# Attention, gated layer and PReLU layer in one launch on one core: the first transfer cut in three, weight sums and low parts placed elsewhere at the attention's end, and the activation written as c + (1 - alpha) max(-c, 0)

## The chip, the cores and the metric

The kernel runs on one core of a Trainium2 chip (trn2). The metric is the device time of one launch in microseconds. In the texts PE is TensorE, ACT is ScalarE, DVE is VectorE, POOL is GpSimd and SP is SyncE, which here only issues transfers.

## The reference

For 2 batches of 12 heads, 448 positions and 64 features each, it computes soft-capped attention, then a gated layer with an RMS norm in front, then a layer with a PReLU, all in float32:

```python
scores = cap * tanh(scale * q @ k.T / cap)
attn = exp(scores - max) / (sum(exp) + 1e-9)
x = (attn @ v)                                  # 896 tokens x 768
xn = x / sqrt(mean(x * x) + 1e-6) * rms_g
x = (silu(xn @ w_gate) * (xn @ w_val)) @ w_out  # 768 -> 1536 -> 768
h = x @ w_in                                    # 768 -> 2048
g = max(h, 0) + alpha * min(h, 0)               # alpha: one number per feature
out = g @ w_out2                                # 2048 -> 768
```

## The kernel before

Each float32 matmul operand of the two layers is split in two float32r tiles, a high part (`wh`, `xh`, cast by ACT) and a low part (`wl`, `xl`, value minus high part, by DVE). A product is then three matmuls: high by high, low weight by high, high weight by low. The matmuls of a layer's first half (L344, and L356 for two weight groups at once) are 128x128 by 128x448.

The first matrix of each layer is multiplied by a seven-product (Strassen-Winograd) scheme. For every weight group g there are products P1 to P7, with the weights A11, A12, A22 and the sums S1 = A21 + A22, S2 = S1 - A11, S3 = A22 - S2, S4 = A12 - S2 (`sum1` to `sum4`, POOL, L115), and the operands B11, B21, B22, T1 to T4 (sums of quarters of the activations, on DVE). A weight tile arrives by an SP transfer into one of 3 `raw` buffers, ACT makes `top` of it (`w_top`, L103), DVE puts both together (`w_bits`, L107), and only then may SP load the next tile into that buffer (`w_next`). `w_hi` (L120, ACT) and `w_lo` (L124, DVE) split a weight.

The order of the work is written out by hand, each engine runs its own list in order, and waits are semaphores. There are four parts:

- The attention (L364 to L451) runs over 12 pairs of heads, 4 steps each: `qk` (PE, L199), `soft` (ACT, L209 and L210), `pv` (PE, L225 and L229). The first pair's queries and keys come in two transfers (L375) and are split by ACT (L386) and DVE (L387 to L389) as they land. DVE then makes the constants `cinv` and `eps_t` (L390 to L396), on which the first `tanh` waits.
- The attention's end (L466 to L490). `recip` makes the reciprocals of the last softmax sums as a high and a low part (`th` L271, `tl` L272), SP spreads each into the tile `r` (L279). `norm` broadcasts them by a matmul into `rps` (L286), DVE scales the attention's output with it (L288, L289), and ACT and POOL sum the squares (L298, L300). `rms` sums them over the partitions (`ms`, L309), and DVE takes the reciprocal root (L313). Between these PE runs P1 and P2 (`product`) of the first two groups of the gated layer, which need batch 0 alone. Then `by_tiles` (L520 to L534) makes T1 in three tiles of 448 columns: `xnorm` (L326), a subtraction, a cast by ACT (L527) and the low part.
- The layers, slot by slot. A slot is one product; the list `hooks` says what the other engines do after its matmuls are issued. The gated layer starts with P5 of groups 0 and 1 together (L356), then P6, P7, P3, P4 of the two groups, one group after the other. Two PSUM pairs of the pool `s` and two of the pool `m` take turns, so P5 and P6 are each in a pair of their own, P7 adds onto P6's after `u2` has read it, and P3 adds onto P5's after `add22` has read it (both are DVE L508).
- The second layer (z) has the PReLU: `prelu_a` makes max(-c, 0) (ACT, L822) and multiplies each half by its alpha (ACT, L825, two instructions), and `prelu_b` takes max(c, 0) minus that (DVE, L828, one instruction of 128x896). Its output goes through `ksplit` (L756 and L508) into the last matrix (f: L593, L595, L597).

Of the kernel before, what the change touches and what calls it, by code (L numbers as in the profile page):

```python
# [56 lines left out]
def attn_moe_kernel(ctx: ExitStack, tc: tile.TileContext, units, qk_in, v, sel, w, gvec, alpha, cap, out):  # L57
# [304 lines left out]
    with tc.manual_schedule():  # L362
# [17 lines left out]
        for t, src in ((g_t, gvec), (al_t, alpha)):  # L380
            nc.sync.dma_start(out=t, in_=src)
        r = raw.pop(0)
        for h, (c0, c1) in enumerate(cuts):
            qc = slice(0, S) if h == 0 else slice(QK - S, QK)
            kc = slice(S, QA) if h == 0 else slice(QA, QK - S)
            nc.scalar.copy(hi[0][:, qc], r[:, qc])  # L386
            nc.vector.tensor_copy(hi[0][:, kc], r[:, kc])  # L387
            nc.vector.tensor_tensor(out=hi[0][D:, kc], in0=r[D:, kc], in1=hi[0][D:, kc], op=ALU.subtract)  # L388
            nc.vector.tensor_tensor(out=q2[0][:, h], in0=r[:, qc], in1=hi[0][:, qc], op=ALU.subtract)  # L389
        nc.vector.reciprocal(out=cinv, in_=cap_t)  # L390
        nc.vector.tensor_scalar_mul(cinv, cinv, QK_SCALE)

# [78 lines left out]
        w_hi(("g", 0, "S1"))  # L471
        w_lo(("g", 0, "S1"))
        first_sum(0, ct("c21"))
        product(pa[1], ("g", 1, "A11"), "B11", True, rows=(0,))
        norm(last - 1)
        norm(last)
        product(pa[1], ("g", 1, "A11"), "B11", True, rows=(1,))
        product(pa[0], ("g", 0, "A12"), "B21", False, rows=(0,))
        w_hi(("g", 1, "S1"))
        rms(B - 1)  # L480
        first_sum(1, ct("c21"))
        c11 = [spare[B - 1][:, :2], xpool.tile([P, 2, S], F32, tag="B22l", name="c11")]
# [24 lines left out]
        def tt(out, a, b, op):  # L507
            nc.vector.tensor_tensor(out=out, in0=a, in1=b, op=op)  # L508
# [8 lines left out]
        def operand_low(name, src):  # L517
            tt(oper[name][1], src, oper[name][0], ALU.subtract)

        def by_tiles(name, i0, out, a, b, fn=None, *args):  # L520

            h, l = (main.tile([P, K3, S], F32R, tag=f"{name}{p}", name=f"x{p}") for p in "hl")
            low = lambda k: tt(l[:, k], out[:, k], h[:, k], ALU.subtract)
            for k in range(K3):
                xnorm(i0 + k)
                tt(out[:, k], a[:, k], b[:, k], ALU.subtract)
                nc.scalar.copy(h[:, k], out[:, k])  # L527
                if k == 1 and fn:
                    fn(*args)
                if k > 0 and not fn:  # L530
                    low(k - 1)
            for k in range(0 if fn else K3 - 1, K3):
                low(k)
            oper[name] = (h, l)  # L534

        i1 = (B - 1) * NP
        by_tiles("T1", i1, x0[:, lo3], x1[:, lo3], x0[:, lo3], w_lo, ("g", 1, "S1"))
        w_hi(("g", 1, "S2"))


# [11 lines left out]
        def pslot(lay, p, g):  # L552

            first = p in ("P1", "P6", "P5")
            wn, xn = OPER[p]

            def pe():
                if first:
                    BANK[p][g] = psum()
                if lay == "g" and p == "P5" and g < 2:  # L560
                    if g == 1:
                        products([pc[0], pc[1]], [("g", 0, "S1"), ("g", 1, "S1")], "T1")
                    return
# [157 lines left out]
            gate(at_["P3"] + 2, g, 1, c12)  # L721


        for g in range(2):
            do(g, 2, w_lo, ("g", g, "S2"))
            do(1 + g, 4, sum3, "g", g)
            do(3 + g, 4, sum4, "g", g)
        do(0, 0, by_tiles, "T2", i1 + K3, x0[:, lo3], x1[:, hi3], x0[:, lo3])

        def later_operands(n0, steps):  # L730
            for name, at_sum, at_hi, out, a, b in steps:
# [72 lines left out]
                        ("B22", 0, 5, b22, None, None), ("T4", 4, 6, b21, b21, b11)))  # L804


        def z_of(g, q):
            if g not in zt:
                zt[g] = block(g)
            return zt[g][:, 2 * q:2 * q + 2, :]  # L810
# [6 lines left out]
            nc.scalar.copy(c11z[g], pa[g][:, :, :S])  # L817

        def prelu_a(g, q, of):
            src, t = of[g][:, :, :S], z_of(g, 0) if q == 0 and g > 1 else (cu if q % 2 else ct)("zn")  # L820
            minus[g, q] = t
            nc.scalar.activation(out=t, in_=src, func=AF.Relu, scale=-1.0)  # L822
            for r in range(2):
                f = q // 2 * (K2N // 2) + 2 * g + r
                nc.scalar.activation(out=t[:, r], in_=t[:, r], func=AF.Copy, scale=al_t[:, f:f + 1])  # L825

        def prelu_b(g, q, of):
            nc.vector.scalar_tensor_tensor(  # L828
                out=z_of(g, q), in0=of[g][:, :, :S], scalar=0.0, in1=minus.pop((g, q)), op0=ALU.max, op1=ALU.subtract
            )  # L830
# [125 lines left out]
```

## Time and profile before

| | |
|---|---|
| median of 3 runs | 611.1 us (610.14 to 617.62) |
| the profiled execution | 616.38 us, of which 614.6 us are the span of its instructions |
| PE busy | 589.5 us, 96% of the span, 2672 matmuls |
| DVE busy | 402.6 us, 66% |
| ACT busy | 357.5 us, 58% |
| POOL busy | 118.7 us, 19% |

The span is the time from the first to the last instruction. A row of a timeline gives the start in us from the span's start, the duration in us, engine, source line, operation, the tile written, the tiles read, the shapes and how many equal instructions are merged; in brackets stands how long the engine was idle before it and what released it. A DVE duration includes time in which the instruction was issued but held up. PE durations overlap, so the rate of matmuls is read from the starts.

### The profile page before, as it was taken

Reading aid. Unit: us, or ns where it says so; the run is one execution under the profiler, and the core shown is the slowest. Engines: PE = TensorE matmul, PEld = TensorE weight load, DVE = VectorE, ACT = ScalarE, POOL = GpSimd, SP = SyncE. Lnnn points to the kernel's source line nnn. Section 1 sums busy time; section 2 is a strip of 40 time slices with the busy share of each in tenths; the row PEclk is TensorE's granted clock in tenths of the full one; section 3 lists DMA queues with packets and bytes.
Section 4 is the critical chain, followed back from the end, with each engine's and each line's share of the span. In section 5 each row is a group of like instructions: output and inputs, shape, how many; then the busy total and the mean of one; then the engine's idle time right before and its main releaser. Section 6 shows DMA issues by size and latency. Waiting matters only on the chain.

```text
span 614.6 us, 6899 instructions
## 1 busy us (share of the span) xinstructions
PE 589.5 (96%) x2672; PEld 503.7 (82%) x2672; DVE 402.6 (66%) x439; ACT 357.5 (58%) x437; POOL 118.7 (19%) x71
## 2 busy tenths in 40 slices
PE   5999988989899999999999999999989999999997
PEld 4666645667799999999999999999979989999996
DVE  7437689967999867766961545679986877614100
ACT  5999878964755455346562542666776887323101
POOL 0013463235003514411000017210451000000000
PEclk9999999999899999999999999999999999999999
DMA  8664642203014434412344264002341344422002
GB/s 294 255 229 159 262 142 86 78 13 145 1 52 153 156 108 149 155 42 85 131 155 155 102 241 171 0 1 67 138 155 52 103 155 136 172 112 81 1 1 90
DMA packets 18632, 73.47 MB, mean 120 GB/s; under 512 B 5672, under 2 KB 6056, under 8 KB 18600
## 3 DMA queue, kind: packets, MB, share of 16 engines
q1 hardware_dynamic: 15592, 72.82, 33.4%
q0 software_dynamic: 2864, 0.21, 0.4%
q8 instruction: 21, 0.34, 0.2%
q14 instruction: 11, 0.09, 0.0%
q10 hardware_dynamic: 144, 0.00, 0.0%
HBM read 70.14 MB, written 2.75 MB: 119 GB/s over the span
## 4 chain that ended last, share of the span: by engine, by line
PE 69%; DVE 7%; issue 3%; DMA 2%; ACT 2%; POOL 0%; SPq 0%; ACTq 0%; DVEq 0%; POOLq 0%
PE s L344 19%; PE m L344 13%; PE s L597 6%; PE s L595 6%; PE s L593 6%; PE m L593 5%; PE m L595 5%; PE m L597 5%; DVE b L508 2%; DMA r<-tl 1%; DVE wl L124 1%; PE ob L229 1%; PE oa L225 1%; PE s L199 1%; DVE b L828 1%
## 5 line engine op out<-in xcount | busy, mean ns | idle before, releaser
L124 DVE TENSOR_TENSOR wl<-wt,wh 128x768 fp32r<-128x768 f32 x98 | 105.9, 1086 | 94.5 <-ACT wh L120 94.2
L115 POOL TENSOR_TENSOR wt<-wt 128x768 f32<-128x768 f32 x40 | 87.8, 2201 | 256.8 <-DVE wt L107 149.3
L120 ACT CAST wh<-wt 128x768 fp32r<-128x768 f32 x98 | 81.3, 833 | 90.6 <-PE s L595 24.7
L103 ACT CAST top<-raw 128x768 f16<-128x768 bf16 x68 | 72.6, 1075 | 44.8 <-DVE wt L107 38.3
L107 DVE SCALAR_TENSOR_TENSOR wt<-raw,top 128x768 uint32<-128x768 uint32 x68 | 67.8, 999 | 8.0 <-ACT top L103 7.6
L344 PE MATMUL s<-xh,wh 128*128 128x448 f32 x234 | 61.8, 372 | 1.0 <-ACT xh L527 1.0
L344 PE MATMUL s<-xh,wl 128*128 128x448 f32 x234 | 61.5, 371 | 1.1 <-DVE wl L124 1.1
L344 PE MATMUL s<-xl,wh 128*128 128x448 f32 x234 | 61.4, 370 | 0.0
L199 PE MATMUL s<-hi 128*128 128x448 f32 x96 | 49.3, 513 | 7.2 <-DVE hi L388 6.6
L593 PE MATMUL s<-ks,wh 128*128 128x448 f32 x176 | 50.6, 367 | 0.8 <-DVE b L828 0.8
L597 PE MATMUL s<-ks,wl 128*128 128x448 f32 x176 | 50.5, 366 | 0.0
L344 PEld LDWEIGHTS s<-xh,wh 128*128 128x128 f32 x234 | 44.3, 190 | 6.3 <-ACT xh L527 1.4
L344 PEld LDWEIGHTS s<-xh,wl 128*128 128x128 f32 x234 | 44.2, 190 | 5.7 <-DVE wl L124 1.3
L209 ACT ACTIVATE pt<-s,cinv 128x896 f32<-128x896 f32 (+1 forms) x48 | 43.6, 908 | 8.6 <-PE s L199 7.2
L344 PEld LDWEIGHTS s<-xl,wh 128*128 128x128 f32 x234 | 44.3, 190 | 4.4
L344 PE MATMUL m<-xh,wh 128*128 128x448 f32 x174 | 45.4, 369 | 1.6 <-ACT b L464 1.6
L210 ACT ACTIVATE pt<-pt,cap_t 128x896 f32<-128x896 f32 (+1 forms) x48 | 45.6, 950 | 1.6
L593 PE MATMUL m<-ks,wh 128*128 128x448 f32 x160 | 45.8, 368 | 0.5 <-DVE b L508 0.5
L597 PE MATMUL m<-ks,wl 128*128 128x448 f32 x160 | 45.8, 367 | 0.0
L344 PE MATMUL m<-xh,wl 128*128 128x448 f32 x174 | 45.2, 368 | 0.0
L344 PE MATMUL m<-xl,wh 128*128 128x448 f32 x174 | 45.2, 368 | 0.0
L229 PE MATMUL ob<-pt,vt 128*128 128x448 f32 x96 | 41.8, 539 | 0.0
(122 smaller groups left out, 977.9 us busy)
## 6 DMA issues: line engine op xcount, KB each, us to landing
raw<-w_in SPq DMA_DIRECT2D x68, 768.0 KB, 4.4
rw<-qk_in SPq DMA_DIRECT2D x11, 928.0 KB, 5.1
vt<-v_in SPq DMA_DIRECT2D x12, 416.0 KB, 5.7
out<-o SPq DMA_DIRECT2D x5, 448.0 KB, 2.5
rw<-qk_in SPq DMA_DIRECT2D x1, 480.0 KB, 4.5
rw<-qk_in SPq DMA_DIRECT2D x1, 448.0 KB, 5.6
out<-o SPq DMA_DIRECT2D x2, 224.0 KB, 2.0
gt<-ea SPq DMA_DIRECT2D x12, 1.8 KB, 1.7
```

Source lines behind the costliest of these rows:

```text
L103: nc.scalar.copy(top_of[u].bitcast(F16)[:, 1::2], raw_t[u].bitcast(BF16)[:, 4:4 * UW + 4:4])
L107: nc.vector.scalar_tensor_tensor(out=f_t[u].bitcast(U32), in0=raw_t.pop(u).bitcast(U32)[:, 1:2 * UW + 1:2], scalar=13, in1=top_of.pop(u), ...
L115: nc.gpsimd.tensor_tensor(out=t, in0=f_t[a], in1=f_t[b], op=op)
L120: nc.scalar.copy(h_t[u], f_t[u].rearrange("p (k m) -> p k m", m=P))
L124: nc.vector.tensor_tensor(out=l_t[u], in0=f_t[u].rearrange("p (k m) -> p k m", m=P), in1=h_t[u], op=ALU.subtract)
L199: nc.tensor.matmul(s[:, n, :S], hi[i][:, S + o:S + o + P], t[hd], start=(m == 0), stop=(m == len(mm) - 1),)
L210: nc.scalar.activation(out=t[:, :n], in_=t[:, :n], func=AF.Exp, scale=cap_t)
L229: nc.tensor.matmul(ob[i][:, :S], lhs, r, start=(h == "T"), stop=(h == "B" and c == 2))
L344: nc.tensor.matmul(ps[:, r, :S], lhs, rhs, start=first and n == 0, stop=n == len(mm) - 1, skip_group_check=True,)
L593: nc.tensor.matmul(dst[l], wh[:, o, :], xh[l], start=first, stop=False)
L595: nc.tensor.matmul(dst[l], wh[:, o, :], xl[l], start=False, stop=False)
L597: nc.tensor.matmul(dst[l], wl[:, o, :], xh[l], start=False, stop=fin)
```

## The change

1. The first pair's queries and keys come in three transfers: queries and the first 256 key columns of head 0, the next 256, the rest. The second has a cast and a subtraction of its own on DVE.
2. At the attention's end `sum3` of the two groups stands on POOL before the last sum of squares, and `sum4` behind it; both stood behind it before. P1 of group 1 is done whole before the last `norm`. `w_lo` of S1, group 1, stands before the reciprocal root.
3. T1 is made whole before its low parts, which follow as one block. T2's first tile comes next, then `w_lo` of S2 for both groups, then T2's other tiles and its low parts. P6 of groups 0 and 1 is done as a pair, as P5 was.
4. The PReLU is c + (1 - alpha) max(-c, 0): DVE turns alpha into 1 - alpha once, ACT makes max(-c, 0) alone, and DVE does the rest in two instructions of 128x448 with the factor as a pointer.

```diff
-        cuts = [(0, QA), (QA, QK)]
+        K0 = S + 2 * P
+        cuts = [(0, K0), (K0, QA), (QA, QK)]
...
-        for h, (c0, c1) in enumerate(cuts):
-            qc = slice(0, S) if h == 0 else slice(QK - S, QK)
-            kc = slice(S, QA) if h == 0 else slice(QA, QK - S)
-            nc.scalar.copy(hi[0][:, qc], r[:, qc])
+        for kc, h, qc in (((S, K0), 0, slice(0, S)), ((K0, QA), None, None), ((QA, QK - S), 1, slice(QK - S, QK))):
+            kc = slice(*kc)
+            if h is not None:
+                nc.scalar.copy(hi[0][:, qc], r[:, qc])
...
         first_sum(0, ct("c21"))
-        product(pa[1], ("g", 1, "A11"), "B11", True, rows=(0,))
+        for g in range(2):
+            sum3("g", g)
+        product(pa[1], ("g", 1, "A11"), "B11", True)
         norm(last - 1)
         norm(last)
-        product(pa[1], ("g", 1, "A11"), "B11", True, rows=(1,))
+        for g in range(2):
+            sum4("g", g)
         product(pa[0], ("g", 0, "A12"), "B21", False, rows=(0,))
         w_hi(("g", 1, "S1"))
+        w_lo(("g", 1, "S1"))
         rms(B - 1)
...
-                if lay == "g" and p == "P5" and g < 2:
+                if lay == "g" and p in ("P5", "P6") and g < 2:
                     if g == 1:
-                        products([pc[0], pc[1]], [("g", 0, "S1"), ("g", 1, "S1")], "T1")
+                        products([BANK[p][0], BANK[p][1]], [("g", i, wn) for i in range(2)], xn)
                     return
...
-        for g in range(2):
-            do(g, 2, w_lo, ("g", g, "S2"))
-            do(1 + g, 4, sum3, "g", g)
-            do(3 + g, 4, sum4, "g", g)
-        do(0, 0, by_tiles, "T2", i1 + K3, x0[:, lo3], x1[:, hi3], x0[:, lo3])
+        def second_operands():
+            low()
+            one2, low2 = tile_maker("T2", i1 + K3, x0[:, lo3], x1[:, hi3], x0[:, lo3])
+            one2(0)
+            for g in range(2):
+                w_lo(("g", g, "S2"))
+            for k in range(1, K3):
+                one2(k)
+            low2()
+
+        do(0, 0, second_operands)
...
+        do(z0 - 6, 5, lambda: nc.vector.tensor_scalar(
+            out=al_t, in0=al_t, scalar1=-1.0, scalar2=1.0, op0=ALU.mult, op1=ALU.add))
...
         def prelu_a(g, q, of):
-            src, t = of[g][:, :, :S], z_of(g, 0) if q == 0 and g > 1 else (cu if q % 2 else ct)("zn")
-            minus[g, q] = t
-            nc.scalar.activation(out=t, in_=src, func=AF.Relu, scale=-1.0)
-            for r in range(2):
-                f = q // 2 * (K2N // 2) + 2 * g + r
-                nc.scalar.activation(out=t[:, r], in_=t[:, r], func=AF.Copy, scale=al_t[:, f:f + 1])
+            t = minus[g, q] = (cu if q % 2 else ct)("zn")
+            nc.scalar.activation(out=t, in_=of[g][:, :, :S], func=AF.Relu, scale=-1.0)
 
         def prelu_b(g, q, of):
-            nc.vector.scalar_tensor_tensor(
-                out=z_of(g, q), in0=of[g][:, :, :S], scalar=0.0, in1=minus.pop((g, q)), op0=ALU.max, op1=ALU.subtract
-            )
+            t = minus.pop((g, q))
+            for r in range(2):
+                f = q // 2 * (K2N // 2) + 2 * g + r
+                nc.vector.scalar_tensor_tensor(
+                    out=z_of(g, q)[:, r], in0=t[:, r], scalar=al_t[:, f:f + 1], in1=of[g][:, r, :S],
+                    op0=ALU.mult, op1=ALU.add
+                )
```

`tile_maker` is `by_tiles` taken apart: it returns one function that makes a tile (`xnorm`, subtraction, cast) and one that makes the three low parts.

The order of the instructions at three places, before and now. First POOL at the attention's end, before: `s2` is the sum of squares, `wt` a weight sum (the first two are `sum3`, the next two `sum4`).

```order
L277 DMA r2_0_84<-tl_931 4x16x28
L300 TENSOR_TENSOR s2_863<-s2_863,sq_997 128x448
L300 TENSOR_TENSOR s2_863<-s2_863,sq_1008 128x448
L300 TENSOR_TENSOR s2_863<-s2_863,sq_1059 128x448
L115 TENSOR_TENSOR wt_401<-wt_578,wt_239 128x768
L115 TENSOR_TENSOR wt_480<-wt_653,wt_314 128x768
L115 TENSOR_TENSOR wt_750<-wt_750,wt_239 128x768
L115 TENSOR_TENSOR wt_832<-wt_832,wt_314 128x768
```

POOL at the same place now:

```order
L277 DMA r2_0_84<-tl_934 4x16x28
L300 TENSOR_TENSOR s2_866<-s2_866,sq_1000 128x448
L300 TENSOR_TENSOR s2_866<-s2_866,sq_1011 128x448
L115 TENSOR_TENSOR wt_404<-wt_581,wt_242 128x768
L115 TENSOR_TENSOR wt_483<-wt_656,wt_317 128x768
L300 TENSOR_TENSOR s2_866<-s2_866,sq_1073 128x448
L115 TENSOR_TENSOR wt_753<-wt_753,wt_242 128x768
L115 TENSOR_TENSOR wt_835<-wt_835,wt_317 128x768
```

The two `sum3` stand directly behind the second sum of squares.

Next DVE where T2 is made, before: `xl` is a low part (the first row that names it still belongs to T2's own), `wl` is `w_lo` of S2 for the two groups.

```order
L326 SCALAR_TENSOR_TENSOR xf<-xf,g_t,spare 128x448
L508 TENSOR_TENSOR xf<-xf 128x448
L326 SCALAR_TENSOR_TENSOR xf<-xf,g_t,spare 128x448
L508 TENSOR_TENSOR xf<-xf 128x448
L508 TENSOR_TENSOR xl<-xf,xh 128x448
L326 SCALAR_TENSOR_TENSOR xf<-xf,g_t,spare 128x448
L508 TENSOR_TENSOR xf<-xf 128x448
L508 TENSOR_TENSOR xl<-xf,xh 128x448 x2
L124 TENSOR_TENSOR wl<-wt,wh 128x768 x2
```

DVE at the same place now:

```order
L326 SCALAR_TENSOR_TENSOR xf<-xf,g_t,spare 128x448
L514 TENSOR_TENSOR xf<-xf 128x448
L124 TENSOR_TENSOR wl<-wt,wh 128x768 x2
L326 SCALAR_TENSOR_TENSOR xf<-xf,g_t,spare 128x448
L514 TENSOR_TENSOR xf<-xf 128x448
L326 SCALAR_TENSOR_TENSOR xf<-xf,g_t,spare 128x448
L514 TENSOR_TENSOR xf<-xf 128x448
L514 TENSOR_TENSOR xl<-xf,xh 128x448 x3
```

The two `w_lo` moved from the end of the block to behind T2's first tile.

Last DVE in the second layer, before: `zn` is what `prelu_a` made, `b` a block of the layer's output.

```order
L124 TENSOR_TENSOR wl<-wt,wh 128x768
L107 SCALAR_TENSOR_TENSOR wt<-raw,top_86 128x768
L828 SCALAR_TENSOR_TENSOR b_2955<-b_2955,zn 128x896
L508 TENSOR_TENSOR b_2955<-m,b_2955 128x896
L124 TENSOR_TENSOR wl<-wt,wh 128x768
L508 TENSOR_TENSOR b_2927<-s,b_2927 128x896
L828 SCALAR_TENSOR_TENSOR b_2927<-b_2927,zn 128x896
L124 TENSOR_TENSOR wl<-wt,wh 128x768
```

DVE at the same place now:

```order
L124 TENSOR_TENSOR wl<-wt,wh 128x768
L107 SCALAR_TENSOR_TENSOR wt<-raw,top_86 128x768
L844 SCALAR_TENSOR_TENSOR b_2959<-zn,al_t,b_2959 128x448 x2
L514 TENSOR_TENSOR b_2959<-m,b_2959 128x896
L124 TENSOR_TENSOR wl<-wt,wh 128x768
L514 TENSOR_TENSOR b_2931<-s,b_2931 128x896
L844 SCALAR_TENSOR_TENSOR b_2931<-zn,al_t,b_2931 128x448 x2
L124 TENSOR_TENSOR wl<-wt,wh 128x768
```

The order is the same; each PReLU row became two instructions of half the size.

## Rows read from the trace of the kernel before

**Rows 1.** A wait of PE (engine, line, waited for: us, times, longest).

```profile
PE rps L286 <- DMA r<-tl: 4.2, 3, 1.8
```

**Rows 2.** Instructions on the first pair's raw tile: ns min/median/max, first and last start.

```profile
L387 DVE CAST hi<-rw x2: 387/408/429, 5.3 to 7.0; 128x512 fp32r<-128x512 f32 x1, 128x448 fp32r<-128x448 f32 x1
L388 DVE TENSOR_TENSOR hi<-rw,hi x2: 623/656/689, 5.8 to 7.4; 64x512 fp32r<-64x512 f32 x1, 64x448 fp32r<-64x448 f32 x1
```

**Rows 3.** Timeline of the start: the first softmax step.

```profile
9.07 1.01 ACT L209 ACTIVATE pt<-s,cinv 128x896 f32<-128x896 f32 x1 [1.37 <-DVE eps_t L396]
```

**Rows 4.** Timeline of the attention's end: from POOL's second sum to its weight sums.

```profile
133.89 1.15 POOL L300 TENSOR_TENSOR s<-s,sq 128x448 f32<-128x448 f32 x1 [0.80 <-ACT sq L298]
...
134.20 0.88 DVE L271 CAST th<-gt 64x28 fp32r<-64x28 f32 x1
...
135.11 0.18 DVE L272 TENSOR_TENSOR tl<-gt,th 64x28 fp32r<-64x28 f32 x1
...
135.97 0.57 SPq L279 DMA_DIRECT2D r<-tl  x1
...
138.12 0.64 PE L286 MATMUL rps<-r,sel_t 128*128 128x448 f32 x2 [1.80 <-DMA r<-tl]
...
141.71 5.43 POOL L115 TENSOR_TENSOR wt<-wt 128x768 f32<-128x768 f32 x3
```

**Rows 5.** Timeline within the attention: a DVE pair beside POOL.

```profile
91.91 3.39 DVE L179 TENSOR_TENSOR q<-rw,hi 128x448 fp32r<-128x448 f32 x2
...
93.51 1.31 POOL L296 TENSOR_TENSOR sq<-xf 128x448 f32<-128x448 f32 x1
```

**Rows 6.** Timeline of PE: P6 of the first group.

```profile
158.45 0.57 PE L344 MATMUL s<-xh,wh 128*128 128x448 f32 x2
...
161.54 1.49 PE L344 MATMUL s<-xh,wl 128*128 128x448 f32 x3 [1.06 <-DVE wl L124]
```

**Rows 7.** Two windows: us, PE, PEld, DVE, ACT, POOL busy (instructions), PEclk, DMA, GB/s.

```profile
162.00:163.00 1.00, 1.00 (x4) 0.87 (x4) 1.00 (x2) 1.00 (x2) 0.00 (x0) 0.50 0.00 0
420.00:441.00 21.00, 21.00 (x104) 19.22 (x103) 20.93 (x20) 14.45 (x20) 6.99 (x3) 1.00 0.34 113
```

**Rows 8.** Timeline of DVE behind P6: u2 and T3's low part, add22 of group 1.

```profile
166.39 1.09 DVE L508 TENSOR_TENSOR b<-s,c 128x896 f32<-128x896 f32 x1 [0.62 <-PE s L344]
...
168.26 1.55 DVE L508 TENSOR_TENSOR xl<-xf,xh 128x1344 fp32r<-128x1344 f32 x1
...
179.51 1.09 DVE L508 TENSOR_TENSOR c<-m,c 128x896 f32<-128x896 f32 x1
```

**Rows 9.** Timeline of PE: the first matmuls of P3, group 1.

```profile
181.07 0.78 PE L344 MATMUL m<-xh,wh 128*128 128x448 f32 x3
```

**Rows 10.** Timelines: two DVE pieces that price a half PReLU.

```profile
12.89 1.16 DVE L179 TENSOR_TENSOR q<-rw,hi 128x448 fp32r<-128x448 f32 x2
...
150.00 0.68 DVE L326 SCALAR_TENSOR_TENSOR xf<-xf,g_t,spare 128x448 f32<-128x448 f32 x1
```

**Rows 11.** Timeline of the second layer: DVE and POOL side by side.

```profile
431.82 1.09 DVE L828 SCALAR_TENSOR_TENSOR b<-b,zn 128x896 f32<-128x896 f32 x1
432.07 2.55 POOL L115 TENSOR_TENSOR wt<-wt 128x768 f32<-128x768 f32 x1 [30.65 <-ACT top L103]
...
433.82 1.61 DVE L124 TENSOR_TENSOR wl<-wt,wh 128x768 fp32r<-128x768 f32 x1
...
449.50 1.40 DVE L828 SCALAR_TENSOR_TENSOR b<-b,zn 128x896 f32<-128x896 f32 x1 [1.23 <-ACT zn L825]
...
452.76 1.08 DVE L508 TENSOR_TENSOR b<-s,b 128x896 f32<-128x896 f32 x1
```

**Rows 12.** Timeline of PE in the second layer and at the last matrix's start.

```profile
454.06 0.79 PE L344 MATMUL s<-xh,wh 128*128 128x448 f32 x3
...
495.49 0.69 PE L593 MATMUL m<-ks,wh 128*128 128x448 f32 x2 [0.51 <-DVE b L508]
```

**Rows 13.** ACT by line and shape, 400 to 530 us: us busy, mean ns.

```profile
L825 ACT ACTIVATE zn<-zn,al_t 128x448 f32<-128x448 f32 x28 | 17.2, 663 | 0.5
```

More of the change, by code (lines that the diff above doesn't have):

```diff
@@ L382, in attn_moe_kernel @@
         r = raw.pop(0)
-        for h, (c0, c1) in enumerate(cuts):
-            qc = slice(0, S) if h == 0 else slice(QK - S, QK)
-            kc = slice(S, QA) if h == 0 else slice(QA, QK - S)
-            nc.scalar.copy(hi[0][:, qc], r[:, qc])
+        for kc, h, qc in (((S, K0), 0, slice(0, S)), ((K0, QA), None, None), ((QA, QK - S), 1, slice(QK - S, QK))):
+            kc = slice(*kc)
+            if h is not None:
+                nc.scalar.copy(hi[0][:, qc], r[:, qc])
             nc.vector.tensor_copy(hi[0][:, kc], r[:, kc])
             nc.vector.tensor_tensor(out=hi[0][D:, kc], in0=r[D:, kc], in1=hi[0][D:, kc], op=ALU.subtract)
-            nc.vector.tensor_tensor(out=q2[0][:, h], in0=r[:, qc], in1=hi[0][:, qc], op=ALU.subtract)
+            if h is not None:
+                nc.vector.tensor_tensor(out=q2[0][:, h], in0=r[:, qc], in1=hi[0][:, qc], op=ALU.subtract)
         nc.vector.reciprocal(out=cinv, in_=cap_t)
@@ L518, in operand_low, with tile_maker, one @@
             tt(oper[name][1], src, oper[name][0], ALU.subtract)
-        def by_tiles(name, i0, out, a, b, fn=None, *args):
+        def tile_maker(name, i0, out, a, b):
             h, l = (main.tile([P, K3, S], F32R, tag=f"{name}{p}", name=f"x{p}") for p in "hl")
-            low = lambda k: tt(l[:, k], out[:, k], h[:, k], ALU.subtract)
-            for k in range(K3):
+            oper[name] = (h, l)
+            def one(k):
                 xnorm(i0 + k)
@@ L527, in by_tiles, with low @@
                 nc.scalar.copy(h[:, k], out[:, k])
[L528 to L534, printed above, removed]
+            def low():
+                for k in range(K3):
+                    tt(l[:, k], out[:, k], h[:, k], ALU.subtract)
+            return one, low
         i1 = (B - 1) * NP
-        by_tiles("T1", i1, x0[:, lo3], x1[:, lo3], x0[:, lo3], w_lo, ("g", 1, "S1"))
+        one, low = tile_maker("T1", i1, x0[:, lo3], x1[:, lo3], x0[:, lo3])
+        for k in range(K3):
+            one(k)
         w_hi(("g", 1, "S2"))
@@ L819, in prelu_a, with prelu_b @@
         def prelu_a(g, q, of):
-            src, t = of[g][:, :, :S], z_of(g, 0) if q == 0 and g > 1 else (cu if q % 2 else ct)("zn")
-            minus[g, q] = t
-            nc.scalar.activation(out=t, in_=src, func=AF.Relu, scale=-1.0)
+            t = minus[g, q] = (cu if q % 2 else ct)("zn")
+            nc.scalar.activation(out=t, in_=of[g][:, :, :S], func=AF.Relu, scale=-1.0)
+        def prelu_b(g, q, of):
+            t = minus.pop((g, q))
             for r in range(2):
                 f = q // 2 * (K2N // 2) + 2 * g + r
-                nc.scalar.activation(out=t[:, r], in_=t[:, r], func=AF.Copy, scale=al_t[:, f:f + 1])
-        def prelu_b(g, q, of):
-            nc.vector.scalar_tensor_tensor(
-                out=z_of(g, q), in0=of[g][:, :, :S], scalar=0.0, in1=minus.pop((g, q)), op0=ALU.max, op1=ALU.subtract
-            )
+                nc.vector.scalar_tensor_tensor(
+                    out=z_of(g, q)[:, r], in0=t[:, r], scalar=al_t[:, f:f + 1], in1=of[g][:, r, :S],
+                    op0=ALU.mult, op1=ALU.add
+                )
         def prelu(n, g, q, of):
```

## The prediction

> **What bounds the kernel now.** I read the table of busy times first: PE is busy for 589.5 of 614.6 us, so about 25 us of the span are left to waiting, and no edit here removes a matmul. The list of PE's waits comes next: which of them the change touches. One is the broadcast `rps`, three times behind the spread of the reciprocal's low part, 4.2 us in all and 1.8 at the longest [rows 1]; others are single waits of about 1 us at P6 of the gated layer [rows 6]. Then the timelines, stage by stage, for what runs ahead of each wait and how long the work behind it can slip. Last the windows: between 162 and 163 us PE did 4 matmuls at a granted clock of 0.50, while 104 matmuls took 21.0 us at a clock of 1.00 in the second layer, 0.20 each [rows 7]. (0.50 is the lower of the two levels, 1.2 GHz.) So three quantities decide: the wait at `rps`, the gaps and the low clock at P6, and in the second layer DVE, which is busy for 20.93 of the 21 us between 420 and 441 [rows 7] and whose delays reach PE.
>
> All sums are made against the profiled execution, 616.38 us, of which 1.8 us lie outside the span. It is 5.3 us above the median of the runs, 611.1; I work out a difference and put it on the median.
>
> **The start (part 1): 0, between -0.2 and +0.2.** The first `tanh` waits not for PE but for DVE's constant `eps_t`, 1.37 us [rows 3]. That constant is last in a DVE chain that begins, for the second piece, around 7.0 us, when the end of the raw tile has landed [rows 2]. A third transfer doesn't make the last one land earlier; it makes the first piece land earlier, and PE's first matmuls with it, which is not what `tanh` waits for. DVE gets a cast and a subtraction more, of half the size: by row 2 a mean cast is 0.41 and a mean subtraction 0.66, so two halves cost some 0.1 each above one whole. This falls into the time in which DVE waits for the last piece.
>
> **The attention's end (part 2): +0.9, between -0.1 and +1.8.** The wait of 1.80 at `rps` starts because P1 of group 1 was cut in two rows of nine matmuls: nine were kept for behind `norm`. Now they stand ahead, 9 x 0.20 = 1.8 us, which fills the wait exactly. But the same nine are missing behind `rps`, where the sum over partitions waits for DVE's scaling, ACT's square and POOL's sum. PE's work is the same and the chain is the same, so the wait moves and nothing is gained; what counts is when `rps` can run.
>
> That is now later. Before, POOL ended its second sum of squares at 133.89 + 1.15 = 135.04. Beside it DVE's cast `th`, of 28 columns, took 0.88, where the subtraction `tl` of the same size just behind took 0.18 [rows 4]: I read 0.7 of it as a hold until POOL let go, since `th` ended at 135.08. The same shows elsewhere: two instructions that take 1.16 together [rows 10] took 3.39 when POOL's square stood between them [rows 5]. Now two `sum3` stand directly behind that second sum on POOL. When it ends, `th` goes, and the `sum3` that is waiting goes ahead of `tl`. One such sum took 5.43 / 3 = 1.8 us [rows 4]. So `tl` begins near 136.7 instead of 135.11 and ends near 136.8. SP's transfer left 0.68 us after `tl`'s end before; I take it that SP was still busy with the transfer of `th` then, and that it now leaves at once. It reached PE 2.15 us after its start (135.97 to 138.12). So `rps` runs at 136.8 + 2.15 = 139.0, 0.9 later than at 138.12 [rows 4]. If the 0.68 is a fixed delay it is +1.6 to +1.8; if `tl` gets in first, about 0 (-0.1 with POOL's order).
>
> **P6 as a pair (part 3): -0.7, between -1.0 and +1.0.** Before, P6 of group 0 ran from 158.45, with a gap in front of its third matmul and one of 1.06 in front of the fourth, which waited for `w_lo` of S2 [rows 6]. The 15 matmuls left then took from 161.54 to 166.39, when `u2` could start [rows 8]: 4.85 us for what takes 3.1 at the full clock, a loss of some 1.7. With `w_lo` of S2 and T2's first tile made earlier, and two groups' matmuls on every tile, I count the gaps and the low clock as gone. The pair, 36 matmuls at 0.20 to 0.21, ends at about 158.45 + 7.4 = 165.9.
>
> The gain does not stay, because DVE has no gap from `u2` to beyond P3 of group 1. `u2` of group 0 had to wait for P6 of group 0 alone; now that ends with the pair, at 165.9 plus a few tenths, so `u2` starts at about 166.07, 0.32 earlier than at 166.39. P7 of group 0 adds onto what `u2` reads and needs T3's low part for its last six matmuls, which ends at 168.26 + 1.55 = 169.8 less 0.32 [rows 8]. So PE, 4 us ahead after P6, stands still in P7. P3 of group 1 began at 181.07 [rows 9], behind `add22`, which ended at 179.51 + 1.09 = 180.60 [rows 8], a slack of 0.47; now `add22` ends at 180.28 and PE may start 181.07 - 180.28 = 0.79 earlier at most. Less what passes between the two engines I take -0.7. The transition as a whole, parts 2 and 3: +0.9 - 0.7 = +0.2.
>
> **The PReLU (part 4): +1.0, between -0.8 and +2.9.** ACT loses two multiplications of 0.66 per PReLU, 28 of them in its list between 400 and 530 us [rows 13]. DVE gets two instructions of 448 columns instead of one of 1.09 for 896 [rows 11]. No row has the new form; the nearest are a pair of 448 columns that took 1.16 together, and a pointer-scaled one of the same kind that took 0.68 by itself, 1.36 for two [rows 10]. The lower end is +0.07 per PReLU, the upper +0.27; I take +0.2, since the single one has the same operands as the new form.
>
> The Trainium skill has a rule against this edit: "VectorE: DVE Perf Modes", section "The DRAIN you can't avoid", says that after each DVE operation the pipe empties before the next one starts, so one long operation beats two short ones. By it the halves cost 2 x 0.68 and the edit +0.27; the pair of 1.16 speaks for the lower end, and the sum would then be 0.4 smaller over the first five PReLUs.
>
> DVE is full around 430 us, so every PReLU pushes what follows: two of them before 431, +0.4. At 431.82 a PReLU of 1.09 begins, and at 432.07 POOL starts a weight sum of 2.55 [rows 11], which the next large DVE instructions but one then had to share with. With a gap between halves POOL gets in there. Before, from the start of the PReLU to the end of `w_lo` it took 433.82 + 1.61 - 431.82 = 3.6; now a half 0.6, POOL's sum of 1.7 to 1.8, a half 0.5, an addition of 1.0 and `w_lo` 0.95 give 4.75: +1.1. Three more PReLUs add 0.4 to 0.5, so DVE is 1.9 late near 447. There a wait of 1.23 for ACT's multiplication stood before [rows 11]; it goes, but the POOL sum that ran in it now holds DVE instead. I therefore keep the whole 1.9 up to the addition `b<-s`, which ended at 452.76 + 1.08 = 453.84 [rows 11], 0.22 ahead of the matmul at 454.06 that needs it [rows 12]: PE is late by 1.9 - 0.2 = 1.7 or 1.8.
>
> At the last matrix's start ACT, without two multiplications (1.3 us), gives its part earlier. PE waits there for DVE, 0.51 at 495.49 [rows 12] and some 0.8 just before; the first goes, the second in part: -0.8. The sum of this part is 1.8 - 0.8 = +1.0. With DVE taking turns well it is -0.8; with the 0.27 and one more sum in the way, +2.9.
>
> **Sum.** 0 + 0.2 + 1.0 = +1.2, so 617.6 us for the profiled execution and 611.1 + 1.2 = 612.3 us for the median.
>
> **Rivals.**
> - *POOL gets in nowhere.* `tl` and both halves go ahead of the waiting sums. Then part 2 is 0, P6 gives -0.7 and the second layer -0.8: together about -1.4, 609.7 us. For it: POOL's own start after a wait isn't instant, and at 135.11 DVE had `tl` out 0.03 after `th` [rows 4]. Against: rows 5, where POOL came between two DVE instructions that had no wait either. Chance 0.27.
> - *Slower: the low clock moves to P7.* The gaps at P6 are exchanged for gaps in P7, while PE stands behind `u2` and T3's low part between 166 and 169.5. Before, gaps of about 1 us each preceded the stretch at 0.50 [rows 6, 7] and cost 1.7. If the clock falls in P7, P3 of group 1 finds no slack and the -0.7 becomes +1.0; with both `sum3` ahead of `th`, `rps` is 1.8 later again. It decides once PE's standstill in P7 is as long as the two gaps together. 611.1 + 1.2 + 1.7 = 614.0, with the second sum 615.8. Chance 0.17.
> - *More or less than is seen.* A wait in the attention or a transfer moved in the second layer, that the reading missed, of several us either way: 0.06.
>
> The forecast has 0.50. The range is 606.5 to 616.5: the bounds of the unknown costs give -1.7 to +5.7, and below I leave some us for the spread of the runs (610.14 to 617.62) and for P7 finding its operands early. About 2%, 12 us, is what a measurement of this kernel can tell from no change; all cases lie inside. Faster by more than that 0.02, within 0.95, slower 0.03.
>
> **What would show each step.** Start: the first `tanh` within 0.2 of 9.07, still released by `eps_t`. End of attention: `tl` a microsecond or more behind `th`, with a POOL sum between, and `rps` near 139.0; PE idle not before `rps` but before the sum over partitions. P6: no wait in front of its matmuls, 36 in 7.5 us, then PE waiting for `u2` and T3's low part. Second layer: pairs of halves of 1.16 to 1.36, one of them with a POOL sum inside, and PE's matmul of 454.06 near 455.8. I am wrong if `rps` is earlier than 138.12, if P7 starts without a wait, or if the pairs take no more than 1.1.

## The result and the profile after

| | before | after |
|---|---|---|
| median of 20 runs | 615.59 us (610.14 to 618.14) | 618.42 us (614.38 to 624.26) |
| the profiled execution | 616.38 us, span 614.6 | 615.77 us, span 614.0 |
| after against before | | 1.0059, 95% interval 1.0033 to 1.0086 |

The change made the kernel slower by 0.6%, 2 to 5 us. The predicted median, 612.3, and the whole range up to 616.5 lie below the measured one, for two reasons: the 611.1 us on which the difference of +1.2 was put was the median of three runs, and twenty give 615.59; and the difference itself is larger than forecast.

The two profiled executions took nearly the same time, so their spans alone would mislead. This is PE's list of waits in the changed kernel (engine, line, waited for: us, times, longest):

```profile
PE rps L286 <- DMA r<-tl: 5.1, 3, 2.9
...
PE s L344 <- DVE b L514: 2.3, 2, 1.4
...
PE ms L309 <- POOL s L300: 1.2, 1, 1.2
PE m L344 <- ACT b L466: 0.8, 1, 0.8
PE s L344 <- DVE xl L514: 0.8, 1, 0.8
```

The longest wait at `rps` is now 2.9 us, where [rows 1] had 1.8, and it is not the one at the attention's end. I then lined up the two traces softmax step by softmax step. The first `tanh` (9.51 against 9.07, [rows 3]) is 0.44 later; the 25th is at 63.91 against 63.52; the 26th at 71.26 against 66.85. Within one step of the attention, which the diff doesn't touch, 4 us were lost. The timeline of that place in the changed kernel:

```profile
58.74 0.18 DVE L272 TENSOR_TENSOR tl<-gt,th 64x28 fp32r<-64x28 f32 x1
58.85 0.94 DVE L107 SCALAR_TENSOR_TENSOR wt<-raw,top 128x768 uint32<-128x768 uint32 x1
...
59.65 1.33 POOL L277 DMA_DIRECT2D r<-tl  x1
59.72 1.11 DVE L175 CAST hi<-rw 128x1856 fp32r<-128x1856 f32 x1
59.82 0.33 SPq L93 DMA_DIRECT2D raw<-w_in  x1
...
68.27 0.71 PE L286 MATMUL rps<-r,sel_t 128*128 128x448 f32 x1 [2.90 <-DMA r<-tl]
...
71.26 1.01 ACT L209 ACTIVATE pt<-s,cinv 128x896 f32<-128x896 f32 x1 [3.90 <-PE s L199]
```

And in the kernel before:

```profile
57.75 0.18 DVE L272 TENSOR_TENSOR tl<-gt,th 64x28 fp32r<-64x28 f32 x1
...
58.24 0.96 DVE L107 SCALAR_TENSOR_TENSOR wt<-raw,top 128x768 uint32<-128x768 uint32 x1 [0.31 <-ACT pt L209]
...
58.66 0.62 POOL L277 DMA_DIRECT2D r<-tl  x1
...
59.12 1.12 DVE L175 CAST hi<-rw 128x1856 fp32r<-128x1856 f32 x1
59.22 0.33 SPq L93 DMA_DIRECT2D raw<-w_in  x1
...
64.48 0.71 PE L286 MATMUL rps<-r,sel_t 128*128 128x448 f32 x1
```

This is the spread of the second group's reciprocals. POOL issues it as two small transfers, `r<-th` and `r<-tl`. Before, DVE paused 0.31 us between `tl` and the weight instruction L107; POOL was nearly through with `r<-tl` (0.62 us) when DVE's cast of 128x1856 began. Now the pause is gone, the cast begins 0.07 us after POOL's issue did, the issue takes 1.33 us, until 60.98, 0.15 us behind the end of that cast. By then SP, which began at 59.82, is at the last of three large loads; before, POOL's issue ended at 59.28, when SP had begun the first. The list of DMA issues (KB, us from issue to landing) shows what that costs, before:

```profile
r<-tl POOLq DMA_DIRECT2D x1, 7.0 KB, 2.1
```

and after:

```profile
rw<-qk_in SPq DMA_DIRECT2D x1, 928.0 KB, 6.4
raw<-w_in SPq DMA_DIRECT2D x1, 768.0 KB, 4.5
vt<-v_in SPq DMA_DIRECT2D x1, 416.0 KB, 7.0
...
r<-tl POOLq DMA_DIRECT2D x1, 7.0 KB, 8.5
```

The three loads land at 64.34, 66.65 and 67.73, and `r<-tl` behind all of them at 68.14.

The Trainium skill, "SBUF — State Buffer", section "SBUF: two separate sides", describes this: descriptors of a transfer issued by POOL are written by POOL itself, which cannot write them while DVE runs a copy in float32 within SBUF, and a transfer issued by SP is free of it. The trace agrees: 1.33 against 0.62 us for the same issue, and its end just behind the cast's.

The rest is in the main as foreseen in kind. The attention's end in the changed kernel:

```profile
139.35 4.44 POOL L115 TENSOR_TENSOR wt<-wt 128x768 f32<-128x768 f32 x2
...
139.46 1.78 DVE L272 TENSOR_TENSOR tl<-gt,th 64x28 fp32r<-64x28 f32 x1
...
141.27 0.57 SPq L279 DMA_DIRECT2D r<-tl  x1
...
143.37 0.64 PE L286 MATMUL rps<-r,sel_t 128*128 128x448 f32 x2 [0.87 <-DMA r<-tl]
...
147.03 1.02 PE L309 MATMUL ms<-s,ones 128*128 128x448 f32 x2 [1.20 <-POOL s L300]
```

`tl` took 0.18 in [rows 4] and takes 1.78, with POOL's sums beside it, and SP's transfer follows at once. Counted from the last `tanh` (126.89 before, 131.24 after), `rps` comes after 11.23 and now after 12.13 us: +0.90. The sum over partitions `ms` follows 3.66 us behind `rps` and waits for POOL; before it came 4.20 behind, directly after 18 matmuls of P1 and P2 and without a wait:

```profile
142.32 0.91 PE L309 MATMUL ms<-s,ones 128*128 128x448 f32 x2
```

In P7 and in the second layer of the changed kernel:

```profile
170.23 1.09 DVE L514 TENSOR_TENSOR b<-s,c 128x896 f32<-128x896 f32 x1 [1.69 <-PE s L356]
...
171.47 0.85 PE L344 MATMUL s<-xh,wh 128*128 128x448 f32 x3 [0.88 <-DVE b L514]
...
173.71 0.88 PE L344 MATMUL s<-xl,wh 128*128 128x448 f32 x3 [0.77 <-DVE xl L514]
...
431.18 2.87 DVE L844 SCALAR_TENSOR_TENSOR b<-zn,al_t,b 128x448 f32<-128x448 f32 x2
...
431.44 2.13 POOL L115 TENSOR_TENSOR wt<-wt 128x768 f32<-128x768 f32 x1 [30.37 <-DVE wt L107]
...
443.25 1.26 DVE L844 SCALAR_TENSOR_TENSOR b<-zn,al_t,b 128x448 f32<-128x448 f32 x2
...
454.85 0.84 PE L344 MATMUL s<-xh,wh 128*128 128x448 f32 x3 [1.39 <-DVE b L514]
```

PE waits in P7 for `u2` and then for T3's low part. A pair of halves takes 1.26 alone and 2.87 with POOL's sum in it, against 1.09 for the whole instruction in [rows 11], and PE waits 1.39 for DVE where it waited for nothing in [rows 12].

Why did the two profiled executions still take the same time? Windows from 300 to 390 us, where neither kernel waits (columns as in [rows 7]), before:

```profile
300.00:390.00 90.00, 90.00 (x437) 81.73 (x436) 44.95 (x43) 38.57 (x43) 14.19 (x6) 1.00 0.43 149
```

and after:

```profile
300.00:390.00 90.00, 90.00 (x446) 83.40 (x445) 47.15 (x46) 39.15 (x44) 14.18 (x6) 1.00 0.44 154
```

At the same granted clock of 1.00 the same matmuls came every 0.2067 us in one execution and every 0.2027 in the other (from their starts). From P3 to the second layer, 1148 matmuls (177.35 to 414.60 before, 180.73 to 413.68 after), that is 237.25 against 232.95 us: 4.3 us in a stretch that the diff leaves alone. The pace may also be why the 20 runs of the kernel before lie in two groups, seven from 610.1 to 611.5 us and thirteen from 613.9 to 618.1; no other execution of it was profiled. So I compare marks counted from the last `tanh`, in profiles of the same pace.

### The profile page after: what moved, and what is told of

Same layout as the page of the kernel before. It is cut to its first block, busy times and chain, and to the rows that moved or that the text cites. A ratio compares the mean times of both kernels' runs of the same rounds, so it can differ in the third digit from the quotient of the medians.

```text
span 614.0 us, 6885 instructions
## 1 busy us (share of the span) xinstructions
PE 587.3 (96%) x2672; PEld 503.5 (82%) x2672; DVE 407.4 (66%) x458; ACT 338.7 (55%) x405; POOL 122.4 (20%) x71
## 4 chain that ended last, share of the span: by engine, by line
PE 70%; DVE 10%; ACT 1%; issue 1%; DMA 1%; POOL 0%; ACTq 0%; DVEq 0%
PE s L344 16%; PE m L344 13%; PE s L603 6%; PE s L605 6%; PE s L601 6%; PE m L601 5%; PE m L605 5%; PE m L603 5%; DVE b L514 2%; DVE b L844 2%; PE ob L229 2%; PE oa L225 2%; PE s L199 2%; DVE wl L124 2%; PE m L356 1%; DVE wt L107 1%
## 5 line engine op out<-in xcount | busy, mean ns | idle before, releaser
L124 DVE TENSOR_TENSOR wl<-wt,wh 128x768 fp32r<-128x768 f32 x98 | 104.5, 1072 | 91.6 <-ACT wh L120 90.5
L115 POOL TENSOR_TENSOR wt<-wt 128x768 f32<-128x768 f32 x40 | 90.8, 2276 | 253.8 <-DVE wt L107 175.7
L107 DVE SCALAR_TENSOR_TENSOR wt<-raw,top 128x768 uint32<-128x768 uint32 x68 | 67.6, 998 | 7.6 <-ACT top L103 7.4
L344 PE MATMUL s<-xh,wh 128*128 128x448 f32 x222 | 57.6, 368 | 2.3 <-DVE b L514 2.3
L344 PE MATMUL s<-xl,wh 128*128 128x448 f32 x222 | 57.1, 366 | 0.8 <-DVE xl L514 0.8
L344 PE MATMUL s<-xh,wl 128*128 128x448 f32 x222 | 57.1, 366 | 0.0
L344 PEld LDWEIGHTS s<-xh,wh 128*128 128x128 f32 x222 | 41.4, 188 | 6.9 <-ACT zn L837 1.7
L344 PEld LDWEIGHTS s<-xl,wh 128*128 128x128 f32 x222 | 41.6, 188 | 4.4 <-DVE xl L514 1.2
L344 PEld LDWEIGHTS s<-xh,wl 128*128 128x128 f32 x222 | 41.6, 188 | 3.7 <-DVE wl L124 0.4
```

Source lines behind the costliest of these rows:

```text
L107: nc.vector.scalar_tensor_tensor(out=f_t[u].bitcast(U32), in0=raw_t.pop(u).bitcast(U32)[:, 1:2 * UW + 1:2], scalar=13, in1=top_of.pop(u), ...
L115: nc.gpsimd.tensor_tensor(out=t, in0=f_t[a], in1=f_t[b], op=op)
L124: nc.vector.tensor_tensor(out=l_t[u], in0=f_t[u].rearrange("p (k m) -> p k m", m=P), in1=h_t[u], op=ALU.subtract)
L344: nc.tensor.matmul(ps[:, r, :S], lhs, rhs, start=first and n == 0, stop=n == len(mm) - 1, skip_group_check=True,)
```

## Experiments

The changed lines are given by their core. In the tables, "ahead" is the number of DVE instructions in the trace, waits among them, ahead of the second group's `tl`.

**1. Three transfers alone (e1), and the change without them (e2).** On the kernel before, part 1 of the diff is put in; in the changed kernel it is taken out.

> The kernel before with part 1 alone (three transfers). Theory M (missed slot): the third transfer delays every later load by about 0.43 us, and at the second spread of the reciprocals, near 59 us, the transfer r<-tl is then issued beside DVE's cast of 128x1856, comes behind the big loads and lands after about 8 us instead of 2. First tanh near 9.5 us (9.07 before), a PE wait of about 2.9 us at that rps, and 4 us more than before: ratio about 1.006 to 1.007. Rival C (chance): the late landing in the changed kernel's profile came from the pace of the loads in that one execution, not from part 1: ratio within 0.2% of 1, r<-tl lands after 2 to 3 us.

> The changed kernel with part 1 undone (two transfers). M: r<-tl at the second spread lands after 2 to 3 us, first tanh near 9.07, and the time is about 4.2 us below the changed kernel, that is 0 to -0.5 us against before (ratio about 0.999 to 1.000). C: as slow as the changed kernel, ratio about 1.006.

**2. The spreads issued by SP (e3 on the changed kernel, e4 on the one before).**

```diff
-            if n < len(members) - 1:
-                nc.gpsimd.dma_start(out=row, in_=x)
-            else:
-                nc.sync.dma_start(out=row.bitcast(F32), in_=x.bitcast(F32))
+            nc.sync.dma_start(out=row.bitcast(F32), in_=x.bitcast(F32))
```

> The changed kernel, with the spreads r<-th and r<-tl issued by SP's queue in all six groups instead of by POOL in five. M: SP issues them ahead of the loads that stand behind them in its list, so no tl lands later than about 3 us after its issue, the 4 us stall at the second rps goes, and the time falls by 4 us or more against the changed kernel (ratio to before about 1.000 or below). C: the late landing has to do with the loads and not with who issues: landings of 6 to 8 us stay, ratio about 1.006.

> The kernel before with the spreads issued by SP in all groups. In the profile of before the tl of the first group landed after 5.4 us, that of the fourth after 6.3 us, and PE waited 4.2 us in all at rps, 1.8 of it at the end. M: these landings fall to 2 to 3 us and the time to 1 to 3 us below before (0.995 to 0.999). C: no change, ratio within 0.2% of 1.

These four left open why the pause is there or not: the third transfer shifts the loads, and it also adds two DVE instructions.

**3. Two idle DVE instructions (e5), and a later load (e6).** e5 on the kernel before, and e6 with the load of `g_t` in front of the first queries and keys:

```diff
+        for _ in range(2):
+            nc.vector.memset(cinv, 0.0)
         r = raw.pop(0)
```

> The kernel before with two tiny DVE instructions (128x1) more at the start, while DVE waits for the first data; the transfers are as before. In the profiles with two transfers DVE paused 0.31 us between tl and the next instruction at the second group, in those with three it didn't, and its cast of 128x1856 then began 0.3 us sooner after tl. Theory I: the pause hangs on how many instructions DVE has behind it (three transfers add two), so here the pause goes, POOL's issue of tl takes 1.3 us instead of 0.62, tl lands after 8 us and the time is 4 us above before (ratio about 1.006), with the first tanh still near 9.07. Theory P: it hangs on the 0.45 us by which the loads come later; then nothing changes here, ratio within 0.2% of 1.

> The kernel before with the small transfer of g_t moved ahead of the first queries and keys, so that all loads come some 0.45 us later without a DVE instruction more. Theory P: tl of the second group lands after 8 us, ratio about 1.007. Theory I: tl lands after 2 us; the time rises by 0.4 us at most, ratio about 1.0005.

**4. Three transfers without a working instruction more (e9), then with DVE's count as before (e11), and the changed kernel with that count (e12).** e9 cuts the transfer in three but keeps the two casts; e11 adds the first line below, e12 puts both into the changed kernel.

```diff
-        nc.vector.memset(rms_b, RMS_EPS)
-        nc.vector.memset(ones, 1.0)
+        nc.gpsimd.memset(rms_b, RMS_EPS)
+        nc.gpsimd.memset(ones, 1.0)
```

> The kernel before with the three transfers of part 1, but DVE's cast and subtraction on the first piece in one, as before (one wait more on DVE, no working instruction more). Theory I (the count of DVE's instructions decides): the pause of 0.3 us in front of DVE's weight instruction near 58 us stays or shrinks with the one wait more; if it stays, POOL's issue of tl takes 0.62 us, it lands after 2 us, and the last tanh starts near 127.3 (126.89 before, 131.2 in the kernels with three transfers so far). Theory T (the third transfer itself does it): issue 1.3 us, landing after 8 us, last tanh near 131.

> The three transfers with one cast for the first piece, as in the run before, but with one of DVE's constants (rms_b) set by POOL, so that DVE again has as many instructions, waits among them, ahead of tl of the second group as before (61 in the trace; 62 in the run before). Theory I: the pause of 0.3 us in front of DVE's weight instruction is back, POOL's issue of tl takes 0.62 us, it lands after 2 us, the last tanh starts near 127.4, and the time is within 1 us of before in executions of like pace. Theory T (the third transfer does it): issue 1.3 us, landing after 8 us, last tanh near 131.

> The changed kernel whole, with two of DVE's constants (rms_b and ones) set by POOL, so that DVE has 61 instructions ahead of that tl instead of 63. Theory I: the pause is back, tl lands after 2 us, the last tanh starts near 127.4 instead of 131.2, and the fastest executions fall from 614.4-616 to about 611-612. Theory T: tl lands after 8 us and nothing changes, 614.4-616.

| kernel | ahead | pause | POOL's issue of tl | lands after | last tanh at | ratio to before, interval |
|---|---|---|---|---|---|---|
| before | 61 | 0.31 | 0.62 | 2.1 | 126.89 | |
| after | 63 | none | 1.33 | 8.5 | 131.24 | 1.0059, 1.0033 to 1.0086 |
| e1 | 63 | none | 1.33 | 8.7 | 131.18 | 1.0042, 1.0001 to 1.0083 |
| e2 | 61 | 0.31 | 0.62 | 2.0 | 127.30 | 1.0015, 0.9976 to 1.0054 |
| e5 | 63 | none | 1.33 | 8.6 | 129.60 | 1.0016, 0.9978 to 1.0054 |
| e6 | 61 | 0.30 | 0.62 | 2.1 | 127.14 | 0.9958, 0.9926 to 0.9991 |
| e9 | 62 | none | 1.33 | 8.6 | 130.68 | 1.0051, 1.0013 to 1.0089 |
| e11 | 61 | 0.31 | 0.62 | 2.1 | 127.87 | 0.9997, 0.9954 to 1.0041 |
| e12 | 61 | 0.31 | 0.62 | 2.1 | 127.29 | 0.9982, 0.9948 to 1.0016 |
| e3 | 63 | none | SP issues | | 124.15 | 0.9980, 0.9941 to 1.0018 |
| e4 | 61 | none | SP issues | | 125.05 | 0.9935, 0.9902 to 0.9968 |

The place in e5, the kernel before with two idle instructions:

```profile
57.38 0.18 DVE L272 TENSOR_TENSOR tl<-gt,th 64x28 fp32r<-64x28 f32 x1
57.49 0.94 DVE L107 SCALAR_TENSOR_TENSOR wt<-raw,top 128x768 uint32<-128x768 uint32 x1
...
58.29 1.33 POOL L277 DMA_DIRECT2D r<-tl  x1
58.36 1.11 DVE L175 CAST hi<-rw 128x1856 fp32r<-128x1856 f32 x1
...
67.03 0.44 PE L286 MATMUL rps<-r,sel_t 128*128 128x448 f32 x1 [2.35 <-DMA r<-tl]
```

And in e12, the whole change with two constants on POOL:

```profile
57.62 0.18 DVE L272 TENSOR_TENSOR tl<-gt,th 64x28 fp32r<-64x28 f32 x1
...
58.10 0.96 DVE L107 SCALAR_TENSOR_TENSOR wt<-raw,top 128x768 uint32<-128x768 uint32 x1 [0.31 <-ACT pt L209]
...
58.52 0.62 POOL L277 DMA_DIRECT2D r<-tl  x1
...
58.98 1.12 DVE L175 CAST hi<-rw 128x1856 fp32r<-128x1856 f32 x1
...
64.32 0.71 PE L286 MATMUL rps<-r,sel_t 128*128 128x448 f32 x1
```

In e5 no transfer is moved, and the stall is there; in e11 and e12 the third transfer is there, and the stall is not. e9 by itself came out as theory T had it; e11 and e12 tell the two theories apart. In all nine kernels in which POOL issues the spread the pause goes by the 61 alone. So among these theory I holds for the pause, the issue and the landing, and e1's first reading, that the 0.43 us by which the loads come later do it, is refuted. Beyond them the number is not enough: in e4, e7, e8 and e10, where SP issues, 61 instructions stand ahead too, and there is no pause. The profile puts the pause down to ACT's `pt`, which cannot be: e5 has the same waits and no pause. What it is was not tried. e6 did not do what it was made for: its first `tanh` came at 8.71, so nothing was delayed. Its ratio of 0.9958 excludes 1, though its last `tanh` comes 0.25 us later than before and no later mark shows a gain; a difference of 0.4% between whole times proves nothing by itself here. The size of the stall varies, from 2.7 us (e5) to 4.35 (after) at the last `tanh`, the later start included. By time alone e5 is unclear: its interval holds 1 as well as the 2.7 us (1.0044) and excludes the 1.006 expected.

e4 confirms the mechanism from the other side and goes beyond it: with SP as issuer the last `tanh` comes 1.8 us earlier than before, and the kernel is 0.65% faster. Step by step, 1.0 of the 1.8 us arises at the 45th `tanh`, behind the fourth spread, which landed after 6.3 us in before and for which PE waited 0.85. Another 1.0 arises at the 33rd: beside a weight sum of POOL, DVE's subtraction L176 took 3.59 us in before; in e4 POOL, with no spread to issue, had done that sum already, and the subtraction took 1.16. The first spread, 5.4 us to landing in before, had cost nothing. e3, at 0.998 where the changed kernel has 1.0059, came out as expected too.

**5. The other parts by themselves, all with SP as issuer:** the PReLU (e7), parts 2 and 3 (e8), and these with the two `sum3` back behind POOL's last sum of squares (e10).

> The kernel before with all spreads on SP's queue (as in the earlier run) and part 4, the PReLU, alone. By the steps of the prediction: PE's matmul of the second layer that came at 454.06 comes 1.8 us later, the last matrix's start gains 0.8, together +1.0 against the earlier run. Rival: the halves are hidden or the shorter ACT work pays for them: 0 to -0.8.

> The kernel before with all spreads on SP's queue and parts 2 and 3 alone (places of the sums and low parts, P6 as a pair). By the steps of the prediction +0.2 against the earlier run with the spreads alone; by what the changed kernel's profile shows, rps 0.9 later but P3 of group 0 0.6 to 1.0 earlier, so -0.6 to -1.0. Rival: with the clock falling in P7's gaps, +1.7.

> The kernel before with all spreads on SP's queue and parts 2 and 3, but with the two sum3 back behind POOL's last sum of squares (part 2 without its POOL order). If POOL's sum holds DVE's tl, tl takes 0.2 us instead of 1.8, the last rps comes 11.1 to 11.3 us after the last tanh instead of 12.2, and P3 of group 0 0.2 to 0.6 us earlier. Rival: w_lo of S2 or something else on DVE sets P3, and nothing behind rps moves.

Marks from the profiles, all four at 0.2027 us per matmul from P3 of group 0 up to the last matrix; the marks of the second layer are the matmuls that stood at 414.60, 454.06 and 496.01 in before.

| us | e4 | e7, PReLU | e8, parts 2 and 3 | e10, sums back |
|---|---|---|---|---|
| last tanh to rps | 11.09 | 11.13 | 12.18 | 11.10 |
| last tanh to P3 of group 0 | 49.28 | 49.32 | 49.53 | 49.14 |
| 414.60 to 454.06 | 39.41 | 41.16 | 39.42 | 39.35 |
| 454.06 to 496.01 | 41.52 | 40.69 | 41.52 | 41.51 |
| ratio to before | 0.9935 | 0.9890 | 0.9918 | 0.9940 |
| interval | 0.9902 to 0.9968 | 0.9846 to 0.9935 | 0.9882 to 0.9954 | 0.9905 to 0.9976 |

The PReLU costs 1.75 and gives back 0.83: +0.92. Parts 2 and 3 cost 1.09 at `rps`, of which +0.25 is left at P3. With the sums back, the same instruction in e8 and in e10 reads, first e8:

```profile
132.75 1.79 DVE L272 TENSOR_TENSOR tl<-gt,th 64x28 fp32r<-64x28 f32 x1
```

then e10:

```profile
132.64 0.18 DVE L272 TENSOR_TENSOR tl<-gt,th 64x28 fp32r<-64x28 f32 x1
```

so POOL's order is what delays `rps`, and it is worth 0.39 us at P3 (49.53 to 49.14). For scale: with the order of before and the clock at 1.00, P3 lies between 49.28 and 49.43 in e1, e4, e5, e6 and e7. The whole times of e4, e7, e8 and e10 do not tell these kernels apart; all four are faster than both kernels of the case. e7 has 6 runs, the others 10 to 12.

## Why the prediction was wrong

- **The start.** The step "The start (part 1): 0, between -0.2 and +0.2" failed. It looked at the first `tanh` alone. That came 0.44 us later in the changed kernel and 0.65 in e1, since the last part landed later and its cast began at 7.44 and 7.65 instead of 7.0 [rows 2]; in e12, with the same three transfers, the cast began at 6.65 and the first `tanh` came 0.35 earlier than before. So this part can go either way. What decides stands 50 us further on: two DVE instructions more take away a pause of 0.31 us, and POOL's small transfer falls behind SP's large ones. That is 2.7 to 4.35 us at the attention's end, where the step had put 0. No rival named it; the nearest was "a wait in the attention ... that the reading missed, of several us either way", with 0.06.
- **The base.** 611.1 was the median of three runs from kernels whose times spread over 8 us. That the profiled execution lay 5.3 us above it was written down and not asked about; in it the matmuls had run at 0.2067 us for most of the way, against 0.2027 in the last matrix. Of the 6.1 us between 612.3 and 618.42, 4.5 are the base and 1.6 are the difference between the medians, 2.8 instead of 1.2. On a base of 615.59 the range would have held the measured median.
- **The attention's end: right at `rps`, wrong behind it.** `rps` +0.9 was forecast, +0.90 and +1.09 measured; `tl` waits for one POOL sum, as the step had it. The rival in which POOL gets in nowhere is refuted by 1.78 against 0.18. But the nine matmuls did gain: the forecast had `ms` waiting for POOL either way, and before it waited for nothing and stood behind the matmuls. With nine of them gone from there it comes 3.66 instead of 4.20 us behind `rps`, and of e8's +1.09 at `rps` only 0.56 is left at `ms`.
- **P6 as a pair: right in the sum, partly by luck.** The transition as a whole was +0.2 in the forecast and +0.25 in e8 against e4. The forecast made it of +0.9 and -0.7. In e8 against e4 it is +1.09 at `rps`, +0.63 at the first matmul of P5, +0.25 at `u2` and +0.25 at P3: about 0.5 was gained where the forecast had nothing, and about 0.4 instead of 0.7 at P6. The reason for the 0.7, `u2` held up by a P6 at the low clock, is not there in e4, where `u2` waits for nothing. For that low clock was not the change's: with the gaps of before the clock fell in e9 (0.67 from 164 to 168) and not in e4 (1.00); with the pair it stayed at 1.00 in e8 and fell in e3:

```profile
168.00:172.00 4.00, 4.00 (x15) 3.63 (x14) 4.00 (x5) 2.01 (x2) 0.00 (x0) 0.67 0.00 0
```

  There P3 came 50.55 us after the last `tanh` instead of 49.53. So the slower rival happens, in some executions, at about 1.0 us instead of the 1.7 that I gave it; its condition, the length of PE's standstill, does not decide it, since PE was busy for 2.44 us from 164 to 168 in e8 and for 2.51 in e3. A low clock at P6 cost as much with the order of before: P3 at 50.25 in e9, 49.28 in e4.
- **The PReLU: right, but for one wait.** +1.7 or +1.8, then -0.8, was forecast; +1.75 and -0.83 measured. A half pair costs 1.26, within 1.16 to 1.36, and POOL's sum goes into the pair at 431. Two halves cost more than the whole (1.09), but the second begins 0.08 us before the first ends (443.85 and 443.92), so the price is the middle of the two that were weighed against each other. By the rule of the Trainium skill named there it would have been 1.36; the trace agrees with it in direction only. At the last matrix's start it is the other wait that goes: the one of 0.8, for the PReLU's own output, is not in the list of waits of the changed kernel, and the one of 0.51 is 0.6 there.
- **The sum.** 0.25 + 0.92 is the forecast's 1.2; with 2.7 to 4.35 for the attention it is 3.9 to 5.5, and the measured interval is 2.0 to 5.3. Without the stall, in e12, the interval is 0.9948 to 1.0016, which just misses the 1.0019 that 1.2 us would be; the 1.2 rest on the marks. That the change stays within 2% of before was given 0.95 and came out so. Two of the forecast's own sums are off and bear on nothing here: its lower bounds add up to -1.9 us without the start, not -1.7, and 0.13 less for each of five PReLUs is 0.65 us, not 0.4.

## What to carry to other kernels

A change that adds an instruction to an engine's list moves everything behind it by little and can still cost much where a small transfer races large ones; look for such a race (a short landing here, a long one there for the same transfer, as in the landings 2.1 and 6.3 us of the kernel before) before calling an edit at the start free. Where it fits, issue small transfers on which a matmul waits from SP's queue and ahead of the large ones, not from POOL beside a busy DVE; here that took 0.65% off the kernel before. And compare two executions only after the rate of their matmuls in a stretch without waits has been read from both.

## What the runs showed of the hardware that I had not expected

- The same instructions on PE ran at two paces, 0.2067 and 0.2027 us per matmul, at a granted clock of 1.00 in both. A pace holds over hundreds of matmuls: in before 0.2067 from about 165 to 427 us and 0.2027 in the last matrix, in the changed kernel 0.2027 from 140 us on. Over 1148 matmuls it is 4.3 us, as much as the stall. What sets it was not tried. Of the profiled executions, the four with the stall ran at 0.2027 there, and of the five without it in which POOL issues the spread, four at 0.2067 and e12 at 0.2027; whether that is chance stays open. The pace does not make up for the stall: the lowest of the 20 runs was 610.14 before and is 614.38 now.
- A pause of 0.31 us in DVE's list came and went with the number of instructions ahead of it (61: there; 62 or 63: gone) in the nine kernels in which POOL issues the spread. With SP as issuer it was absent at 61 too (e4, e7, e8, e10). What it is stays open.
- While PE stood still for the late spread its clock fell, in the changed kernel

```profile
66.00:70.00 4.00, 1.73 (x5) 1.59 (x6) 0.95 (x2) 1.36 (x2) 0.00 (x0) 0.78 0.69 213
70.00:74.00 4.00, 4.00 (x14) 2.88 (x13) 3.90 (x4) 2.71 (x3) 3.48 (x2) 0.79 0.47 160
```

  but not in e9, where the same wait was 2.50 us and the clock 1.00 in both windows. Between the 25th and the 26th `tanh` e9 lost 2.3 us against before, and e5, e1 and the changed kernel, with 0.72, 0.77 and 0.78 from 66 to 70 us, lost 2.8, 3.6 and 4.0. The clock may be a part of why the stall is not of one size; this was not tried.
